# A planned attention and gated feed-forward kernel on one core: weight conversion tied to a row-sum step, and other GpSimd durations in the plan

## The chip, the cores and the metric

The kernel runs on one core of a Trainium2 chip. The metric is the device time in microseconds of one execution, from the runs shown below. One execution was also taken with the hardware profiler, and all rows below come from it.

## The reference

Causal attention over 4 batches, 12 heads, 448 positions and head size 64 gives x with 1792 rows and 768 columns. A feed-forward part follows, with a gate between two matrix products. All data are float32.

```python
scores = q @ k.transpose(0, 1, 3, 2) / sqrt(64)
scores = where(triu(ones((448, 448)), k=1), -1e9, scores)
p = exp(scores - scores.max(-1)); attn = p / (p.sum(-1) + 1e-9)
x = (attn @ v).transpose(0, 2, 1, 3).reshape(1792, 768)
h = x @ w_in                      # 768 x 2048
g = h * clip(h + 3, 0, 6) / 6
out = g @ w_out                   # 2048 x 768
```

## The kernel before

**Groups.** The 1792 positions are worked off in five groups. Group 0 holds the first 112 positions of all four batches (448 columns). Groups 1 to 4 hold the other 336 positions of one batch each. The feed-forward part of a group can start when the attention of its six head pairs is done: every product of its first half reads all six x tiles.

**Attention of group 0** (`first_pair`, six of them, called p = 0 to 5; the row sums of each are its "sums"). For each pair of heads TensorE adds a mask (L321) and the scores (L328), VectorE takes the row maximum (L335, for the second head first), one head's exponential with its row sums is done on ScalarE in four pieces (L347), and the other head goes over VectorE (L355), ScalarE (L359) and a VectorE sum (L362). `inverse` (L368, L369) turns the row sums of both heads into factors, GpSimd multiplies them in (L376), TensorE transposes (L385), ScalarE or VectorE copy the result out (pt), TensorE multiplies by v (L398), and `x_split` writes x as a rounded part xh and a rest xl (ScalarE L237 for xh and for a copy xf; GpSimd or VectorE L249 for xl).

**Attention of the other groups** (`pair`) has the scores (L424), mask and maximum in one VectorE instruction (L441), the exponential (L448), `inverse` (L457, L458), the scaling on GpSimd (`scaled`, L470), transposes (L481) and the product with v (L500).

**Weights** (`weights`). There are 40 chunks: 16 of w_in with 768 columns (three matrix products for each of six 128-column pieces, 18 in all), then 24 of w_out with 512 columns (12 products each). The host sends them as pairs of 32-bit words of a 64-bit array. In group 0 VectorE turns a chunk into float32 with three instructions on half a chunk of 768 columns or on a whole one of 512 (`one_by_one`, L536, L538, L541), by way of a PSUM bank "s" (six banks, shared with the attention). The result wf goes to device memory (`kept`), from which groups 1 to 4 load it. Every chunk is split into wh (ScalarE, L237) and wl (L249, GpSimd or VectorE). The tiles wd (raw words) have 4 buffers, wf, wh and wl 3 each.

**Order.** No order is written out. `Flow` plans it before the program is built: each operation has a key, a list of engines it may run on with a factor on its duration and a lag after which that engine may take it, and the tiles it reads and writes. An engine that is free takes the ready operation with the lowest key whose buffers are free. The resulting order of each engine is then fixed in the program; on the chip every instruction waits for its real inputs. So a duration in the plan is no delay on the chip, it only moves places in the queues. The keys of group 0 that matter here: first pair p starts at -66 + 8p, the sums have that +3.5; the conversion of chunk i has 3i - 9 + .01; the pairs of group 1 start at 4 + 13n.

Of the kernel before, what the change touches and what calls it, by code (L numbers as in the profile page):

```python
# [38 lines left out]
B, H, S, D = 4, 12, 448, 64  # L39
DM, DFF = 768, 2048  # L40
C = 112
NC_ = S // C
R = S - C
NPAIR = H // 2
# [5 lines left out]
T_FIRST, T_EARLY, T_REST, T_LOAD, T_W, T_WLOAD = -66, 4, -16, -24, 9, 9  # L50
# [3 lines left out]
    gh=1, gl=1, prow=3, wf=3, xf=2, r=2, ob=2, qr=3, kr=3, vr=3, wh=3, wl=3, pr3=4, pr2=4, pr1=4,  # L54
# [135 lines left out]
def tile_causal_attention_hardswish_moe(ctx: ExitStack, tc: tile.TileContext, q, k, v, w_in, w_out, out):  # L190
# [11 lines left out]
    flow = Flow({**BUFS, **BANKS})  # L202
# [16 lines left out]
    def one(key, ways, dur, emit, r, w):  # L219

        ways = {e: x if isinstance(x, tuple) else (x, 0) for e, x in ways.items()}
        flow.op(key, ways, [(dur, emit, w)], r)
# [53 lines left out]
    def x_split(key, g, p, av, n):  # L276
        xh, xl = buf("xh", [128, S], F32R), buf("xl", [128, S], F32R)
        x_t[g, p] = xh, xl
        move(key, n, lambda: ap(xh)[:, :n], lambda: ap(av)[:, :n], [(av, 0)], [(xh, 0)], {"A": 1, "D": (1, .5)})
        y = av  # L280
        if g < 2:
            y = buf("xf", [128, S])
            move(key, n, lambda: ap(y)[:, :n], lambda: ap(av)[:, :n], [(av, 0)], [(y, 0)], {"A": 1})
        minus(
            key + .01, n, lambda: ap(xl)[:, :n], lambda: ap(y)[:, :n], lambda: f(ap(xh)[:, :n]),
            [(y, 0), (xh, 0)], [(xl, 0)], {"P": 2, "D": (1, 1.0)} if g < 2 else {"D": 1},
        )


# [6 lines left out]
    def first_pair(p):  # L296
        t = T_FIRST + 8 * p
# [71 lines left out]
            nc.vector.reciprocal(r, r)  # L369

        sums = [(st, 0, 4)] + [(st, 1, 4 + b) for b in range(B)]
        one(t + 3.5, {"D": 1}, .5, inverse, [], sums)
        for e in (1, 0):
            one(
                t + 4, {"P": 1}, 1.05,
                lambda _, e=e: nc.gpsimd.tensor_tensor(  # L376
                    pb[e](), pb[e](), wide(e, 4), ALU.mult
                ),
# [30 lines left out]
    def pair(n):  # L409
        b, p = divmod(n, NPAIR)  # L410
        t = T_REST + 16 * n if b else T_EARLY + 13 * n
# [48 lines left out]
        sums = [(st, e, 4 + i) for e in range(2) for i in TILES]  # L460
        one(t + 4, {"D": 1}, .45, inverse, [], sums)
        pt = {}
        for e in range(2):
            for i in reversed(TILES):
                def scaled(g, e=e, i=i):
                    x, r = ap(pr[e, i]), ap(st)[:, e, 4 + i:5 + i]
                    if g == "A":
                        nc.scalar.activation(x, x, ACTF.Copy, scale=r)
                    else:
                        nc.gpsimd.tensor_scalar(x, x, r, 1.0, ALU.mult, ALU.mult)  # L470
                one(
                    t + 4.5 + .1 * e, {"P": 1}, (C * (i + 1) + 300) / 1100, scaled,
                    [(st, e, 4 + i)], [(pr[e, i], 0)],
                )
            for a, js in enumerate(((0,), (1,), (2, 3))):
                blocks = [(i, j) for j in js for i in range(max(j, 1), NC_)]
                tp, ph = bank("s"), buf(f"pt{js[0]}", [C, S] if js[0] == 0 else [C, R])

                def turn(e=e, blocks=blocks, tp=tp):
                    for o, (i, j) in enumerate(blocks):  # L480
                        nc.tensor.transpose(ap(tp)[:C, C * o:C * o + C], ap(pr[e, i])[:, C * j:C * j + C], ident)  # L481

                key = t + 6 + 3 * e + a
                pe(key, [(.3, turn, [(tp, 0)])], [(pr[e, i], 0) for i in {i for i, _ in blocks}])
                move(
                    key + .1, R, lambda ph=ph: ap(ph)[:, :R], lambda tp=tp: ap(tp)[:C, :R],
                    [(tp, 0)], [(ph, 0)], {"A": 1, "D": (1, .4)} if b else {"A": 1},
                )
                o = 0
                for j in js:  # L490
                    w = R if j == 0 else S - C * j
                    pt[e, j] = ph, o, w
                    o += w
# [18 lines left out]
    def weights(g, i, t, early):  # L512

        n = cols(i)
        wd, wh, wl = buf("wd", [128, 1536], I32), buf("wh", [128, 768], F32R), buf("wl", [128, 768], F32R)
        if g:
            dma(t - T_W - T_WLOAD, 512 * n, lambda: f(ap(wd))[:, :n], lambda: kept[i, :, :n], [("kept", i)], [(wd, 0)])
            w, wk = lambda: f(ap(wd))[:, :n], [(wd, 0)]
        else:
            m, r = divmod(i - NF, 4)  # L520
            src = w_in[i] if i < NF else w_out[m, :, 4 * r:4 * r + 4]
            dma(
                early if early else t - T_W - T_WLOAD, 1024 * n,
                lambda: ap(wd)[:, :2 * n].rearrange("p (n k) -> p n k", k=256), lambda: src, [], [(wd, 0)],
            )
            wf = buf("wf", [128, 768])
            w = lambda: ap(wf)[:, :n]

            def bits(cv, o, m, step):
                ti = ap(cv)[:, :m].bitcast(I32)
                low, high = (ap(wd)[:, 2 * o + a:2 * o + 2 * m:2] for a in range(2))
                if step == 0:
                    nc.vector.tensor_scalar(ti, high, 3, 0x3FFFFFFF, ALU.logical_shift_left, ALU.bitwise_and)  # L536
                elif step == 1:
                    nc.vector.scalar_tensor_tensor(ti, high, -(1 << 30), ti, ALU.bitwise_and, ALU.bitwise_or)  # L538
                else:
                    o = ap(wf)[:, o:o + m].bitcast(I32)  # L540
                    nc.vector.scalar_tensor_tensor(o, low, 29, ti, ALU.logical_shift_right, ALU.bitwise_or)  # L541

            wk = []
            m = n if n <= 512 else n // 2
            for o in range(0, n, m):
                cv = bank("s")
                wk.append((wf, o))
                one_by_one = [
                    (elem(m), lambda _, cv=cv, o=o, a=a: bits(cv, o, m, a), [[(cv, 0)], [(cv, 0)], [(wf, o)]][a])
                    for a in range(3)  # L550
                ]
                flow.op(t - T_W + .01, {"D": (1, 0)}, one_by_one, [(wd, 0)])
            dma(t - T_W, 512 * n, lambda: kept[i, :, :n], w, wk, [("kept", i)])
        move(t - T_W + .1, n, lambda: ap(wh)[:, :n], w, wk, [(wh, 0)], {"A": 1})
        minus(
            t - T_W + .2, n, lambda: ap(wl)[:, :n], w, lambda: f(ap(wh))[:, :n], wk + [(wh, 0)], [(wl, 0)],
            {"D": 1.15, "P": (2, .5)} if g else {"P": 2, "D": (1.15, 2.0)},
        )
        return wh, wl
# [7 lines left out]
    def group(g):  # L567
# [3 lines left out]
        for i in range(NF):  # L571
            t = t0 + 3 * i
            wh, wl = weights(g, i, t, -900 + 4 * i + 11 if not g and i < 4 else None)
            acc, r = bank("mo"), buf("r", [128, S])
            for part in range(3):
                def products(part=part, wh=wh, wl=wl, acc=acc):
                    for c in (2 * part, 2 * part + 1):
                        xh, xl = (ap(x)[:, :n] for x in x_t[g, c])
                        triple(ap(acc)[:, :n], n, wh, wl, c, xh, xl, c == 0, c == NK - 1)
                cs = (2 * part, 2 * part + 1) if g else range(NK)  # L580
                xs = [(x, 0) for c in cs for x in x_t[g, c]]
                pe(t + part, [(step, products, [(acc, 0)])], [(wh, 0), (wl, 0)] + xs)
            t -= 4
            one(
                t, {"A": 1}, (n + 300) / 1200,
                lambda _, r=r, acc=acc: nc.scalar.activation(  # L586
                    ap(r)[:, :n], ap(acc)[:, :n], ACTF.Relu, bias=three, scale=1.0
                ),
                [(acc, 0)], [(r, 0)],
            )  # L590
            def gate(_, r=r, acc=acc):
                nc.vector.scalar_tensor_tensor(ap(r)[:, :n], ap(r)[:, :n], 6.0, ap(acc)[:, :n], ALU.min, ALU.mult)  # L592

            one(t, {"D": 1}, elem(n), gate, [(acc, 0)], [(r, 0)])
            move(
                t, n, lambda i=i: ap(gh)[:, i, :n], lambda r=r: ap(r)[:, :n], [(r, 0)], [(gh, i)],
                {"P": 1.05, "A": (1, .3)} if g else {"A": 1},
            )
            minus(
                t, n, lambda i=i: ap(gl)[:, i, :n], lambda r=r: ap(r)[:, :n], lambda i=i: f(ap(gh)[:, i, :n]),  # L600
                [(r, 0), (gh, i)], [(gl, i)], {"D": 1, "P": (1.9, .7)} if g else {"P": 2, "D": (1, 1.5)},
            )
        for m in range(NK):
            acc, ob = bank("mo"), buf("ob", [128, S])
# [70 lines left out]
```

## Time and profile before

| | us |
|---|---|
| three runs | 676.68, 678.63, 911.4 |
| their median | 678.63 |
| the profiled execution | 676.35 |
| its span (first to last instruction) | 674.6 |
| TensorE busy in the span | 656.7 (97%) |
| VectorE busy | 419.5 (62%) |
| ScalarE busy | 360.6 (53%) |
| GpSimd busy | 236.2 (35%) |

PE stands for TensorE, DVE for VectorE, ACT for ScalarE, POOL for GpSimd. A row of a timeline has the start, the duration, the engine, the line of the program, the operation, output and inputs, and in brackets how long the engine stood idle before it and who ended that. 911.4 is far from the other two runs; the profiled execution is close to them.

### The profile page before, as it was taken

What the parts mean: (1) busy time and instruction counts of PE and PEld (TensorE: products, weight loads), DVE (VectorE), ACT (ScalarE), POOL (GpSimd) and SP (SyncE); (2) the same over time, 40 slices, a digit from 0 to 9 for tenths busy, and PEclk for the clock granted to TensorE, in tenths of its full rate; (3) what the DMA queues carried; (4) which work ended last, traced back from release to release, by engine and by line L of the source; (5) the groups of instructions that cost most, each with busy time, mean ns of one, the idle gap of its engine ahead of it and who ended that gap; (6) DMA issues with size and microseconds to landing.
All of it is one profiled execution on the core that took longest, in us unless ns stands there. A gap on an engine that the chain in (4) does not pass through costs nothing.

```text
span 674.6 us, 11883 instructions
## 1 busy us (share of the span) xinstructions
PE 656.7 (97%) x4236; PEld 573.5 (85%) x4236; DVE 419.5 (62%) x881; ACT 360.6 (53%) x859; POOL 236.2 (35%) x294
## 2 busy tenths in 40 slices
PE   6789999999999999999999999999999999999998
PEld 4558888778888888988988889988898989999997
DVE  5889979995755657444467563455667443466432
ACT  3575666555454556555556565555466654444432
POOL 1556877536651335302242252220335302022000
PEclk7869999999999999999999999999999999999999
DMA  9988777787874343444644335555342334643452
GB/s 225 287 273 241 255 237 229 240 294 236 286 216 146 107 137 114 127 140 130 205 133 131 112 93 161 151 165 176 109 134 85 95 102 133 210 141 111 141 164 70
DMA packets 60347, 113.63 MB, mean 168 GB/s; under 512 B 14976, under 2 KB 26880, under 8 KB 60288
## 3 DMA queue, kind: packets, MB, share of 16 engines
q1 hardware_dynamic: 60288, 112.88, 55.9%
q8 instruction: 33, 0.54, 0.3%
q14 instruction: 26, 0.21, 0.1%
HBM read 94.77 MB, written 18.09 MB: 167 GB/s over the span
## 4 chain that ended last, share of the span: by engine, by line
PE 89%; DVE 4%; POOL 2%; DMA 1%; SPq 1%; issue 1%; ACT 1%; DVEq 0%; ACTq 0%
PE mo L563 24%; PE mo L564 22%; PE mo L565 22%; PE s L424 7%; PE s L500 7%; PE s L481 6%; POOL pr L470 2%; DMA gh<-in_k_dram 1%; SPq L228 1%; DVE s L538 1%; DVE s L536 1%; DVE wl L249 1%; PE s L398 1%; DVE prow L335 0%; PE mo L385 0%
## 5 line engine op out<-in xcount | busy, mean ns | idle before, releaser
L249 DVE TENSOR_TENSOR wl<-wd,wh 128x512 fp32r<-128x512 f32 (+1 forms) x160 | 136.8, 856 | 136.0 <-ACT wh L237 135.7
L237 ACT CAST wh<-wd 128x512 fp32r<-128x512 f32 (+1 forms) x160 | 112.7, 705 | 128.1 <-PE mo L564 78.2
L563 PE MATMUL mo<-xh,wh 128*128 128x336 f32 (+1 forms) x480 | 162.8, 339 | 0.0
L563 PE MATMUL mo<-gh,wh 128*128 128x336 f32 (+1 forms) x480 | 161.6, 337 | 0.0
L565 PE MATMUL mo<-gh,wl 128*128 128x336 f32 (+1 forms) x480 | 156.7, 326 | 0.0
L564 PE MATMUL mo<-gl,wh 128*128 128x336 f32 (+1 forms) x480 | 156.4, 326 | 0.0
L565 PE MATMUL mo<-xh,wl 128*128 128x336 f32 (+1 forms) x480 | 156.4, 326 | 0.0
L564 PE MATMUL mo<-xl,wh 128*128 128x336 f32 (+1 forms) x480 | 156.3, 326 | 0.0
L470 POOL TENSOR_SCALAR pr<-pr,prow 112x224 f32<-112x224 f32 x144 | 98.4, 700 | 118.9 <-PE mo L564 108.6
L563 PEld LDWEIGHTS mo<-xh,wh 128*128 128x128 f32 x480 | 90.1, 188 | 11.7 <-issue 8.8
L244 POOL TENSOR_SCALAR gh<-r 128x336 fp32r<-128x336 f32 x58 | 30.4, 525 | 196.1 <-DVE r L592 175.0
L448 ACT ACTIVATE pr<-s,prow 112x448 f32<-112x448 f32 (+1 forms) x144 | 76.9, 541 | 41.4 <-DVE prow L441 41.2
L563 PEld LDWEIGHTS mo<-gh,wh 128*128 128x128 f32 x480 | 90.2, 188 | 9.7 <-issue 6.7
L565 PEld LDWEIGHTS mo<-gh,wl 128*128 128x128 f32 x480 | 90.2, 188 | 1.5
L564 PEld LDWEIGHTS mo<-gl,wh 128*128 128x128 f32 x480 | 90.3, 188 | 1.3
L565 PEld LDWEIGHTS mo<-xh,wl 128*128 128x128 f32 x480 | 90.1, 188 | 1.5
L564 PEld LDWEIGHTS mo<-xl,wh 128*128 128x128 f32 x480 | 90.3, 188 | 1.1
L441 DVE CUSTOM_DVE_ANT_0 s<-s,mask 112x448 f32<-112x448 f32 (+1 forms) x144 | 69.4, 534 | 21.4 <-PE s L424 21.4
L249 POOL TENSOR_TENSOR wl<-wf,wh 128x512 fp32r<-128x512 f32 (+1 forms) x36 | 54.7, 1519 | 43.2 <-ACT wh L237 41.5
L237 ACT COPY pt<-s 112x336 f32<-112x336 f32 x140 | 53.4, 444 | 23.6 <-PE s L481 23.3
L424 PE MATMUL s<-kr,qr 64*112 64x448 f32 (+2 forms) x288 | 56.8, 492 | 0.5 <-ACT xf L237 0.5
L586 ACT ACTIVATE r<-mo,three 128x336 f32<-128x336 f32 (+1 forms) x80 | 44.5, 557 | 19.7 <-PE mo L565 15.8
(59 smaller groups left out, 674.6 us busy)
## 6 DMA issues: line engine op xcount, KB each, us to landing
wd<-kept_w SPq DMA_DIRECT2D x64, 384.0 KB, 3.3
wd<-kept_w SPq DMA_DIRECT2D x96, 256.0 KB, 2.6
wd<-in_w_in_dram SPq DMA_DIRECT2D x16, 768.0 KB, 5.4
wd<-in_w_out_dram SPq DMA_DIRECT2D x24, 512.0 KB, 5.3
kept_w<-wf SPq DMA_DIRECT2D x16, 384.0 KB, 5.6
kept_w<-wf SPq DMA_DIRECT2D x24, 256.0 KB, 5.6
kr<-in_k_dram SPq DMA_DIRECT2D x24, 224.0 KB, 3.6
vr<-in_v_dram SPq DMA_DIRECT2D x24, 224.0 KB, 3.2
```

Of the source, the lines that this page charges most:

```text
L237: nc.scalar.copy(o(), i()) if scale is None else nc.scalar.mul(o(), i(), scale)
L249: (nc.gpsimd if e == "P" else nc.vector).tensor_tensor(o(), a(), b(), ALU.subtract)
L424: nc.tensor.matmul(ap(ps[e, i])[:C, :w], ap(qr)[m, C * (i - 1):C * i], ap(kr)[m, :w], start=True, stop=True)
L441: lambda _, e=e, i=i, w=w, dst=dst: nc.vector.tensor_tensor_reduce(dst(), dst(), mask[:, S - w:], -0.125, 3.0e38, ALU.add, ALU.min, ap(st) ...
L448: lambda _, e=e, i=i, dst=dst: nc.scalar.activation(ap(pr[e, i]), dst(), ACTF.Exp, bias=ap(st)[:, e, i:i + 1], scale=-1.0, accum_out=ap(st ...
L470: nc.gpsimd.tensor_scalar(x, x, r, 1.0, ALU.mult, ALU.mult)
L481: nc.tensor.transpose(ap(tp)[:C, C * o:C * o + C], ap(pr[e, i])[:, C * j:C * j + C], ident)
L500: nc.tensor.matmul(ap(av)[64 * e:64 * e + 64, R - w:R], ap(vr)[:, j, e, :], ap(ph)[:, o:o + w], start=(j == 0), stop=(j == NC_ - 1),)
L563: nc.tensor.matmul(ps, ap(wh)[:, a], xh, start=start, stop=False)
L564: nc.tensor.matmul(ps, ap(wh)[:, a], xl, start=False, stop=False)
L565: nc.tensor.matmul(ps, ap(wl)[:, a], xh, start=False, stop=stop)
L586: lambda _, r=r, acc=acc: nc.scalar.activation(ap(r)[:, :n], ap(acc)[:, :n], ACTF.Relu, bias=three, scale=1.0),
```

## The change

The `inverse` step of first pair p now counts as the writer of a name ("sums", p). The conversion of every chunk but chunk 0 now counts as a reader of ("sums", 5), so that the plan lets it onto VectorE only once the sums of the last first pair stand before it. No tile is shared between the two, so that the chip itself has no new wait; the order of the queues alone is changed. Five planned durations are changed as well: the xl of groups 0 and 1 on GpSimd (factor 2 to 2.4), the scaling on GpSimd (`scaled`: for 224, 336 and 448 columns from .48, .58, .68 to .65, .87, .95 us), and the rest gl of the gate, on VectorE and GpSimd, with a longer lag before GpSimd may take it in groups 1 to 4.

```diff
@@ x_split
-            [(y, 0), (xh, 0)], [(xl, 0)], {"P": 2, "D": (1, 1.0)} if g < 2 else {"D": 1},
+            [(y, 0), (xh, 0)], [(xl, 0)], {"P": 2.4, "D": (1, 1.0)} if g < 2 else {"D": 1},
@@ first_pair
-        one(t + 3.5, {"D": 1}, .5, inverse, [], sums)
+        one(t + 3.5, {"D": 1}, .5, inverse, [], sums + [("sums", p)])
@@ pair
-                    t + 4.5 + .1 * e, {"P": 1}, (C * (i + 1) + 300) / 1100, scaled,
+                    t + 4.5 + .1 * e, {"P": 1}, min(.95, .2 + C * (i + 1) / 500), scaled,
@@ weights
-                flow.op(t - T_W + .01, {"D": (1, 0)}, one_by_one, [(wd, 0)])
+                flow.op(t - T_W + .01, {"D": (1, 0)}, one_by_one, [(wd, 0)] + ([("sums", NPAIR - 1)] if i else []))
@@ group
-                [(r, 0), (gh, i)], [(gl, i)], {"D": 1, "P": (1.9, .7)} if g else {"P": 2, "D": (1, 1.5)},
+                [(r, 0), (gh, i)], [(gl, i)], {"D": 1.4, "P": (2.6, 1.0)} if g else {"P": 2.3, "D": (1.4, 1.5)},
```

## Rows read from the trace of the kernel before

**Rows 1.** The page: busy tenths of TensorE and its granted clock, 40 slices.

```profile
PE   6789999999999999999999999999999999999998
...
PEclk7869999999999999999999999999999999999999
```

**Rows 2.** Busy time by stretch (us, busy of each engine with count, clock, DMA).

```profile
29.00:51.00 22.00, 15.82 (x93) 9.69 (x94) 19.89 (x48) 14.29 (x44) 11.79 (x11) 0.69 0.91 272
51.00:110.00 59.00, 59.00 (x321) 50.51 (x322) 52.15 (x114) 35.22 (x76) 42.51 (x37) 1.00 0.77 238
...
200.00:670.00 470.00, 468.93 (x3137) 421.49 (x3135) 257.18 (x540) 250.88 (x576) 118.62 (x173) 1.00 0.45 133
```

**Rows 3.** Who TensorE waited for, whole span (total us, times, longest).

```profile
PE s L398 <- ACT pt L237: 4.1, 3, 2.8
...
PE s L481 <- POOL pr L470: 1.1, 4, 0.3
```

**Rows 4.** Timeline of VectorE, 27 to 42 us.

```profile
27.11 1.19 DVE L368 TENSOR_SCALAR prow<-prow 112x8 f32<-112x8 f32 x1
...
30.57 0.55 DVE L536 TENSOR_SCALAR s<-wd 128x384 int32<-128x384 int32 x1
...
32.23 0.62 DVE L249 TENSOR_TENSOR xl<-xf,xh 128x448 fp32r<-128x448 f32 x1
32.76 0.62 DVE L335 TENSOR_REDUCE prow<-s 112x4 f32<-112x448 f32 x1
...
35.50 0.55 DVE L536 TENSOR_SCALAR s<-wd 128x384 int32<-128x384 int32 x1
...
40.47 0.61 DVE L362 TENSOR_REDUCE prow<-pr 112x4 f32<-112x448 f32 x1
41.11 0.17 DVE L368 TENSOR_SCALAR prow<-prow 112x8 f32<-112x8 f32 x1
```

**Rows 5.** Timeline of ScalarE, 33 to 39 us.

```profile
33.70 0.35 ACT L347 ACTIVATE pr<-s,prow 112x112 f32<-112x112 f32 x1 [1.86 <-DVE prow L341]
...
37.77 0.58 ACT L359 ACTIVATE pr<-pr 112x448 f32<-112x448 f32 x1
```

**Rows 6.** Timeline of TensorE, 27 to 51 us, and one row of 95 us.

```profile
27.91 1.04 PE L328 MATMUL s<-gh 64*112 64x112 f32 x16 [0.32 <-DMA gh<-in_k_dram]
...
34.62 1.76 PE L398 MATMUL s<-pt,gl 112*64 112x112 f32 x16 [2.81 <-ACT pt L237]
...
37.24 2.96 PE L424 MATMUL s<-kr,qr 64*112 64x448 f32 x8
...
41.35 0.99 PE L398 MATMUL s<-pt,gl 112*64 112x112 f32 x16 [0.62 <-ACT pt L237]
...
46.66 1.76 PE L398 MATMUL s<-pt,gl 112*64 112x112 f32 x16 [0.62 <-ACT pt L237]
48.35 2.61 PE L424 MATMUL s<-kr,qr 64*112 64x448 f32 x8
50.89 0.47 PE L563 MATMUL mo<-xh,wh 128*128 128x448 f32 x1
...
95.25 1.57 PE L424 MATMUL s<-kr,qr 64*112 64x448 f32 x8
```

**Rows 7.** Timeline of GpSimd, 26 to 28 us.

```profile
26.43 1.84 POOL L249 TENSOR_TENSOR wl<-wf,wh 128x768 fp32r<-128x768 f32 x1 [3.19 <-ACT wh L237]
```

**Rows 8.** Timeline of VectorE: the last instruction of chunk 14's conversion.

```profile
106.15 0.55 DVE L541 SCALAR_TENSOR_TENSOR wf<-wd,s 128x384 int32<-128x384 int32 x1
```

**Rows 9.** Timeline of TensorE: the first product of chunk 14, counted from 50.89 us.

```profile
113.04 0.37 PE L563 MATMUL mo<-xh,wh 128*128 128x448 f32 x1
```

**Rows 10.** Groups of instructions by line and shape (busy us, mean ns | idle before).

```profile
L470 POOL TENSOR_SCALAR pr<-pr,prow 112x448 f32<-112x448 f32 x48 | 43.3, 901 | 0.0
...
L237 ACT CAST wh<-wf 128x768 fp32r<-128x768 f32 x16 | 13.3, 831 | 12.9 <-PE mo L564 11.9 <-DVE wf L541 0.9
...
L249 POOL TENSOR_TENSOR xl<-xf,xh 128x448 fp32r<-128x448 f32 x5 | 6.5, 1293 | 5.0 <-ACT xf L237 5.0
```

## Prediction

> **What bounds the kernel now.** I read the page first. TensorE is at nine tenths or more from the fourth slice on, and the granted clock is at full from the fifth [rows 1]. The table by stretch says the same in numbers: from 51 to 110 us TensorE is busy 59.00 of 59.00 us, and from 200 to 670 us 468.93 of 470.00, at clock 1.00 [rows 2]. After 51 us there is almost nothing to win. The reader is to see that the open time lies ahead of that: from 29 to 51 us TensorE is busy 15.82 of 22.00 us at a mean clock of 0.69, while VectorE is busy 19.89 [rows 2].
>
> The waits of TensorE name who ended its idle time: a pt copy on ScalarE, 4.1 us in three waits, the longest 2.8 [rows 3]. That is no ScalarE problem. In its timeline the exponentials of the last first pair (p = 5) waited 1.86 us for VectorE's L341 until 33.70, and the copy stands behind them [rows 5]. So the third view is VectorE's timeline from 27 to 42 us. The scores of p = 5 are done at 27.91 + 1.04 = 28.95 [rows 6], yet the first of their maxima starts at 32.76, behind a half chunk of conversion from 30.57 to 32.23 and an xl [rows 4]. Three more halves fill 35.50 to 40.47, and only then comes L362, the last row sum, with `inverse` at 41.11 [rows 4]. The first feed-forward product follows at 50.89 [rows 6], 9.78 us later.
>
> **The barrier, part by part.** It takes four half conversions (chunks 1 and 2) from in front of the last sums. One half is 32.23 - 30.57 = 1.66 us, four are 6.64. Chunk 0 stays where it was.
>
> The first half stands alone on the way: without it the maximum starts at 31.1, the exponentials at 33.70 - 1.66 = 32.04, the copy and the product with v behind them equally earlier. The other three are partly hidden. The input of L362 comes from L359, which ScalarE ran from 37.77 to 38.35 [rows 5]; of the three halves only 40.47 - 38.35 = 2.12 stands after that. If ScalarE keeps its order, L359 moves by 1.66 to 36.11 and L362 starts at 36.7: the sums come 1.66 + 2.12 = 3.8 us earlier. If the plan lets L359 run as soon as its input is there (L355 would end near 33.9), the sums come at about 35.2, which is 5.9 earlier. I take 3.8, because the copies that stand ahead of L359 are those of earlier pairs with lower keys (xh of p = 3 has -27.5, L359 of p = 5 has -24). Lower end: 2.1, with another VectorE step or a blocked one in front.
>
> Such a block is in the rows. L368 takes 0.17 us at 41.11, but 1.19 at 27.11, when GpSimd was in a wl from 26.43 to 28.27 [rows 4, 7]. The Trainium skill, "SBUF — State Buffer", section "Who interferes with whom", says that a two-port VectorE instruction and a GpSimd one share a port pair and the second to come waits for the whole of the first; the trace agrees (1.02 us lost). By that rule the last `inverse` may lose the same 1.0 if it falls into an xl on GpSimd, and the gain at the sums would be 2.8.
>
> From the sums to the first product I leave the 9.78 us as they are (scaling, transposes, copy, product with v, xh, xf, xl, in series). So the feed-forward begins near 47.1, 3.8 earlier (2.1 to 5.9). For this to be a gain, the pair products that TensorE runs in between (L424 at 37.24 and 48.35, rows 6) must still fit in; VectorE is free there and fewer banks "s" are taken by conversions, so I count on it.
>
> **What the wait puts off.** Behind the sums now queue the conversions of chunks 1 to 39 and, with each, its write to `kept` on SyncE's queue, the load of a later chunk into the same wd, ScalarE's wh and the wl. After 37.3 the first two chunks cost 6.64 us and end at 43.9 at best, against 40.47 before: a lag of 3.4 us. What hides it is the lead of the conversions. Counted chunk by chunk (18 products for each), the lead is about 10 us for most of the 40 and least for chunk 14: converted at 106.70, first used at 113.04 [rows 8, 9], 6.34 us. From the end of a conversion wh (0.83) and wl (1.84) must follow, 2.9 us with the handing over [rows 7, 10]. Free of cost are thus 6.34 - 2.9 = 3.4 us. VectorE has 59.00 - 52.15 = 6.85 us idle between 51 and 110 us [rows 2], so the lag can be worked off before chunk 14, but TensorE comes 3.8 earlier: 0.4 short if the lag is gone, 3.8 short if none is (then the whole gain is gone). VectorE's idle time is partly waits of its own; I charge 0.9.
>
> **The durations in the plan.** These add no instruction. Measured are 1.29 us for the xl of 448 columns and .90 for the scaling of 448 [rows 10]; the plan had 1.25 and .68 and now has 1.50 and .95. So they err on the long side now. What they can bring is bounded by what TensorE still waits for GpSimd, 1.1 us in four waits [rows 3]. What they can cost is a gl moved to the other engine: hidden, since from 200 to 670 us VectorE is busy 257.18 and GpSimd 118.62 of 470 us [rows 2]. A worse order could cost as much as the four waits, 1.1. I take a gain of 0.3.
>
> **Sum.** -3.8 + 0.9 - 0.3 = -3.2 on the profiled 676.35, which is 673.15. The two runs that lie close to it are 676.68 and 678.63, 0.3 and 2.3 higher, so I add 0.4: 673.5 us. With the bounds of the parts: -5.9 - 1.1 + 0 = -7.0 gives 669.7; -2.1 + 3.4 + 1.1 = +2.4 gives 679.2.
>
> **Rivals.**
> *Filler falls back.* The sums move up, but the pair products that now stand between 37 and 51 us go behind the first chunks. Twelve products of the first pair and eight of the second are about 1.57 us per eight at full clock [rows 6], some 3.6 us in all; then 3.8 - 3.6 leaves nothing: 676.8. The same time comes out if ScalarE's or GpSimd's order, not VectorE's, holds the sums, and the barrier doesn't do what it says. For it: ScalarE had 4.1 us of TensorE's waits. Against it: these waits go back to VectorE, as shown.
>
> *Dense start.* The granted clock there is 0.69. After the wait of 2.81 us, L398 takes 1.76 us where the same work took 0.99 at 41.35; L424 took 2.96 and 2.61 where 1.57 is the time at full clock [rows 6]. Over L398 twice and L424 twice that is .77 + .77 + 1.39 + 1.04 = 4.0 us at the lower of the two levels. If the stage closes up so far that most of its idle 22.00 - 15.82 = 6.2 us and this excess go, up to 10.2 us come back; two thirds of it give 669.9, all 666.5, so I price it at 668. The Trainium skill, "TensorE: Matmul & The Clock Gate", section "What's actually happening", says that the low clock is the default and sustained activity lifts it; that a low stretch follows the 2.81 us wait agrees. Against it: the last scores wait for a DMA until 27.91 whatever VectorE does.
>
> *Starved feed-forward (slower).* The sums gain little, for instance by blocked VectorE steps, and the four halves are pure lag on an engine that is 88% busy. If 6.64 us of lag stay up to chunk 14, the lead of 6.34 turns to -0.3, and TensorE waits 2.9 + 0.3 = 3.2 us there: 679.6. A wait of 2.81 us was followed by a slow L398 and a slow L424, .77 + 1.39 = 2.2 us more [rows 6]: 681.8. I price it at 681. It decides from a lag of 3.4 us at chunk 14. Against it: the 6.85 us of idle VectorE.
>
> **How the numbers follow.** Forecast 0.52, filler falls back 0.20, dense start 0.12, starved 0.13, and 0.03 for an order that I don't foresee. The range reaches to the priced end of the dense start and to just short of the starved case's: 667.5 to 680.5. A measurement of this kernel tells about 2%, 13.6 us, from no change. The ceiling of 10.2 us is below that, and so is the starved case; faster by over 2% 0.03, within 0.94, slower 0.03.
>
> **What would show it.** Right: no L536 between chunk 0 and the last L362; `inverse` of p = 5 near 37 instead of 41.1; the first L563 near 47; TensorE full from there. Clock from 29 to 47 us above 0.69. If chunk 14 or a neighbour makes TensorE wait for wl, wh or wf, the starved case is at work. If L563 starts early with more L424 behind it than before, the filler fell back. The forecast is wrong if another engine's order turns out to hold the last sums, or if the new order delays pairs and chunks in later groups, where TensorE now waits for almost nothing.

## The result and the profile after

The changed kernel takes 669.0 us (667.65 to 671.1, four runs) beside 677.65 before. Of the four runs behind 677.65 one took 911.4 us and is left out of the ratio, which is 0.9886 with a 95% interval from 0.9842 to 0.993. Timed a second time beside some of the experiments it took 669.19, ratio 0.9893 (0.9875 to 0.9911). By this second ratio the change makes the kernel 7.2 us or 1.1% faster. The time is inside the stated range, and the gain is more than twice the 3.2 us that the prediction added up. Its profiled execution took 668.97 us with a span of 667.3.

The page of the changed kernel answers to [rows 1]:

```profile
PE   7689999999999999999999999999999999999998
...
PEclk9989999999999999999999999999999999999999
```

The clock is now at nine tenths or more in all slices but the third. Busy time by stretch, as in [rows 2], and the stretch from 29 to 60 us:

```profile
29.00:51.00 22.00, 17.61 (x116) 13.45 (x117) 19.66 (x45) 13.76 (x38) 14.92 (x12) 0.84 0.92 281
51.00:110.00 59.00, 58.78 (x320) 48.54 (x320) 55.13 (x119) 35.79 (x80) 37.76 (x37) 1.00 0.78 238
...
200.00:663.00 463.00, 463.00 (x3107) 417.53 (x3106) 255.32 (x546) 251.09 (x577) 109.16 (x157) 1.00 0.45 134
...
29.00:60.00 31.00, 26.40 (x158) 21.24 (x159) 28.31 (x63) 18.75 (x49) 21.46 (x17) 0.89 0.91 278
```

TensorE's waits, as in [rows 3]:

```profile
PE mo L385 <- POOL pr L376: 4.1, 4, 2.4
...
PE s L398 <- ACT pr L448: 1.8, 1, 1.8
...
PE mo L563 <- DVE r L592: 0.2, 1, 0.2
```

The 1.1 us that TensorE waited for the scaling on GpSimd in the later groups have gone. VectorE, as in [rows 4]:

```profile
29.14 0.61 DVE L249 TENSOR_TENSOR xl<-xf,xh 128x448 fp32r<-128x448 f32 x1
29.68 0.62 DVE L335 TENSOR_REDUCE prow<-s 112x4 f32<-112x448 f32 x1
...
34.44 0.61 DVE L362 TENSOR_REDUCE prow<-pr 112x4 f32<-112x448 f32 x1
35.09 0.17 DVE L368 TENSOR_SCALAR prow<-prow 112x8 f32<-112x8 f32 x1
...
35.41 0.54 DVE L536 TENSOR_SCALAR s<-wd 128x384 int32<-128x384 int32 x1
```

ScalarE, as in [rows 5]:

```profile
33.56 0.60 ACT L359 ACTIVATE pr<-pr 112x448 f32<-112x448 f32 x1
36.19 0.53 ACT L237 CAST xh<-s 128x448 fp32r<-128x448 f32 x1 [2.03 <-PE s L398]
```

TensorE, as in [rows 6]:

```profile
32.02 2.96 PE L424 MATMUL s<-kr,qr 64*112 64x448 f32 x8
...
39.15 0.64 PE L424 MATMUL s<-kr,qr 64*112 64x224 f32 x4
...
42.11 1.64 PE L398 MATMUL s<-pt,gl 112*64 112x112 f32 x16 [1.80 <-ACT pr L448]
43.68 0.74 PE L563 MATMUL mo<-xh,wh 128*128 128x448 f32 x1
```

What to see: no conversion stands among the VectorE steps of the last first pair; the last `inverse` starts at 35.09 instead of 41.11; L359 goes ahead of xh, the order that I had not taken; the first feed-forward product starts at 43.68 instead of 50.89, 7.21 us earlier. It does so with 12 pair products (L424) ahead of it, where before had 20; the missing eight are 1.57 us of work at full clock [rows 6], so coming 7.21 us earlier is worth 5.6. From the first product on, TensorE's idle time is 0.22 + 0.44 + 0 = 0.66 us (51 to 110, 110 to 200 and 200 to 663 us) against 0.49 + 1.07 = 1.56 before. The sum of 5.6 and 0.9 is 6.5 of the 7.3 by which the spans differ.

By the trace alone the story of the prediction would pass: the barrier freed the sums, the clock and the idle time came back as in its "dense start". The experiments say otherwise about what freed the sums.

### The profile page after: what moved, and what is told of

Same layout as the page of the kernel before. It is cut to its first block, busy times and chain, and to the rows that moved or that the text cites. A ratio compares the mean times of both kernels' runs of the same rounds, so it can differ in the third digit from the quotient of the medians.

```text
span 667.3 us, 11888 instructions
## 1 busy us (share of the span) xinstructions
PE 650.2 (97%) x4236; PEld 569.6 (85%) x4236; DVE 419.3 (63%) x890; ACT 364.3 (55%) x869; POOL 222.2 (33%) x275
## 4 chain that ended last, share of the span: by engine, by line
PE 92%; DVE 4%; DMA 1%; ACT 1%; issue 1%; POOL 1%; SPq 0%; DVEq 0%; POOLq 0%; ACTq 0%
PE mo L563 25%; PE mo L564 23%; PE mo L565 23%; PE s L424 8%; PE s L500 7%; PE s L481 6%; DVE s L538 1%; DVE s L536 1%; DMA gh<-in_k_dram 1%; DVE wf L541 1%; POOL pr L376 1%; PE s L398 0%; PE s L328 0%; DVE prow L335 0%; PE mo L385 0%
## 5 line engine op out<-in xcount | busy, mean ns | idle before, releaser
L249 DVE TENSOR_TENSOR wl<-wd,wh 128x512 fp32r<-128x512 f32 (+1 forms) x156 | 131.3, 841 | 146.7 <-ACT wh L237 146.5
L563 PE MATMUL mo<-xh,wh 128*128 128x336 f32 (+1 forms) x480 | 163.3, 340 | 0.2 <-DVE r L592 0.2
L563 PE MATMUL mo<-gh,wh 128*128 128x336 f32 (+1 forms) x480 | 161.2, 336 | 0.0
L470 POOL TENSOR_SCALAR pr<-pr,prow 112x224 f32<-112x224 f32 x144 | 100.6, 715 | 125.8 <-PE mo L564 112.7
L448 ACT ACTIVATE pr<-s,prow 112x448 f32<-112x448 f32 (+1 forms) x144 | 77.3, 542 | 40.8 <-DVE prow L441 40.8
L563 PEld LDWEIGHTS mo<-xh,wh 128*128 128x128 f32 x480 | 90.4, 188 | 9.8 <-issue 5.4
L563 PEld LDWEIGHTS mo<-gh,wh 128*128 128x128 f32 x480 | 90.2, 188 | 9.6 <-issue 6.9
L244 POOL TENSOR_SCALAR gh<-r 128x336 fp32r<-128x336 f32 x51 | 25.8, 506 | 188.5 <-DVE r L592 172.7
L441 DVE CUSTOM_DVE_ANT_0 s<-s,mask 112x448 f32<-112x448 f32 (+1 forms) x144 | 70.2, 531 | 26.4 <-PE s L424 26.4
L249 POOL TENSOR_TENSOR wl<-wf,wh 128x512 fp32r<-128x512 f32 (+1 forms) x33 | 50.1, 1518 | 39.8 <-ACT wh L237 32.2
L586 ACT ACTIVATE r<-mo,three 128x336 f32<-128x336 f32 (+1 forms) x80 | 44.6, 557 | 24.7 <-PE mo L565 24.7
L424 PE MATMUL s<-kr,qr 64*112 64x224 f32 (+2 forms) x288 | 54.4, 483 | 0.0
```

The lines of the kernel that those rows point to most:

```text
L249: (nc.gpsimd if e == "P" else nc.vector).tensor_tensor(o(), a(), b(), ALU.subtract)
L424: nc.tensor.matmul(ap(ps[e, i])[:C, :w], ap(qr)[m, C * (i - 1):C * i], ap(kr)[m, :w], start=True, stop=True)
L441: lambda _, e=e, i=i, w=w, dst=dst: nc.vector.tensor_tensor_reduce(dst(), dst(), mask[:, S - w:], -0.125, 3.0e38, ALU.add, ALU.min, ap(st) ...
L448: lambda _, e=e, i=i, dst=dst: nc.scalar.activation(ap(pr[e, i]), dst(), ACTF.Exp, bias=ap(st)[:, e, i:i + 1], scale=-1.0, accum_out=ap(st ...
L563: nc.tensor.matmul(ps, ap(wh)[:, a], xh, start=start, stop=False)
L586: lambda _, r=r, acc=acc: nc.scalar.activation(ap(r)[:, :n], ap(acc)[:, :n], ACTF.Relu, bias=three, scale=1.0),
```

## The experiments

All were timed beside the kernel before, whose medians on the three occasions were 676.12, 676.32 and 676.51. Gains against the kernel before are named by the ratio, differences between two of the other kernels by their medians; the two ways differ by up to 0.9 us (the durations alone gain 3.1 us by the ratio and 3.6 by the medians). "Idle" is TensorE's idle time from 29 us to the last product, "clock" its mean granted clock from 29 to 60 us. "Loss" is idle plus 31 us times the shortfall of the clock; it is a rough account, since it counts a low clock also where TensorE is idle. "L424" counts the pair products ahead of the first L563. Idle, clock and moments are of one profiled execution each. The same kernel's moments differ by about 1 us between executions (the last inverse of the changed kernel at 35.09 and at 36.23).

| kernel | median us | ratio (95%) | last inverse | first L563 | L424 | idle | clock | loss |
|---|---|---|---|---|---|---|---|---|
| before | 676.3 | 1 | 41.1 | 50.9 | 20 | 7.7 | .78 | 14.5 |
| barrier alone | 675.58 | .9993 (.9977 to 1.0009) | 39.9 | 44.5 | 12 | 8.7 | .83 | 13.9 |
| durations alone | 672.49 | .9954 (.9937 to .9972) | 37.0 | 44.5 | 12 | 8.1 | .89 | 11.5 |
| changed, chunk 1 free | 672.61 | .9952 (.9937 to .9968) | 37.5 | 44.5 | 12 | 8.2 | .83 | 13.5 |
| changed, chunk 0 bound too | 671.68 | .9947 (.9921 to .9973) | 37.6 | 43.2 | 12 | 5.3 | .89 | 8.7 |
| xl factor alone | 673.91 | .9961 (.9946 to .9976) | 36.8 | 43.4 | 12 | 6.6 | .82 | 12.2 |
| barrier and xl factor | 671.56 | .9922 (.9902 to .9943) | 36.5 | 45.1 | 12 | 6.5 | .89 | 9.9 |
| changed, old xl factor | 673.41 | .9946 (.9928 to .9964) | 39.9 | 44.5 | 12 | 7.6 | .83 | 12.9 |
| barrier, mask first | 671.68 | .9926 (.9909 to .9943) | 40.2 | 48.6 | 24 | 6.3 | .83 | 11.5 |
| changed, again | 669.19 | .9893 (.9875 to .9911) | 36.2 | 43.8 | 12 | 6.7 | .94 | 8.6 |
| changed, mask first | 669.05 | .9890 (.9873 to .9908) | 36.2 | 45.8 | 24 | 5.6 | .94 | 7.5 |
| durations, mask first | 670.48 | .9911 (.9895 to .9928) | 38.0 | 48.7 | 20 | 5.9 | .86 | 10.2 |
| changed, late conversion | 667.29 | .9866 (.9846 to .9885) | 36.0 | 44.0 | 20 | 4.0 | .94 | 5.9 |

The profiled times minus the loss lie between 659.6 and 662.4 us for all of these kernels, while the times themselves spread over 9.3 us. So TensorE's idleness and low clock behind 29 us account for most of the differences; the moment of the last sums alone does not ("barrier, mask first" has it at 40.2, and its median is 4.6 us below that of the kernel before).

**Barrier alone.** The durations as before:

```diff
+        one(t + 3.5, {"D": 1}, .5, inverse, [], sums + [("sums", p)])
+                flow.op(..., one_by_one, [(wd, 0)] + ([("sums", NPAIR - 1)] if i else []))
```

> The barrier without the five changed durations. Theory A (the barrier brings the last sums forward, and nearly all of the gain lies ahead of the first feed-forward product): the last inverse near 35 to 36 us instead of 41.1, the first L563 near 44 to 45 instead of 50.9, 670 to 671 us; the waits of TensorE for GpSimd in the later groups (1.1 us) come back. Theory B (the durations do it, by another order on GpSimd and ScalarE): little change, 675 to 677. Theory C (the granted clock of the start differs from execution to execution and makes up much of the difference): 671 to 674, with a time that follows the mean clock of the runs.

No change that can be measured. That sinks theory A for the barrier by itself. Theory C, the granted clock of each execution, can be judged by the runs on record. Of the 47 runs of the kernel before that were timed beside the experiments, the 15 with a mean granted clock of 0.99 or more have a median of 675.0 us, the other 32 one of 676.6. The five runs of the changed kernel on the last occasion all have 0.99 or more and a median of 669.19, so that 5.8 us of its gain are left at a like clock. It is not shown whether the rest is chance or the higher clock is itself brought by the change. With the barrier alone the nine runs at 0.99 or more have a median of 675.6, no gain at all. VectorE of this kernel:

```profile
33.14 0.58 DVE L355 TENSOR_TENSOR pr<-s,prow 112x448 f32<-112x448 f32 x1
35.18 0.62 DVE L240 CAST xh<-s 128x448 fp32r<-128x448 f32 x1 [1.46 <-PE s L398]
36.93 0.63 DVE L441 CUSTOM_DVE_ANT_0 s<-s,mask 112x448 f32<-112x448 f32 x1 [1.13 <-PE s L424]
...
39.25 0.61 DVE L362 TENSOR_REDUCE prow<-pr 112x4 f32<-112x448 f32 x1
39.90 0.17 DVE L368 TENSOR_SCALAR prow<-prow 112x8 f32<-112x8 f32 x1
...
50.73 0.51 DVE L441 CUSTOM_DVE_ANT_0 s<-s,mask 112x336 f32<-112x336 f32 x1
...
51.51 0.60 DVE L536 TENSOR_SCALAR s<-wd 128x384 int32<-128x384 int32 x1
...
54.45 0.55 DVE L541 SCALAR_TENSOR_TENSOR wf<-wd,s 128x384 int32<-128x384 int32 x1
54.92 0.61 DVE L592 SCALAR_TENSOR_TENSOR r<-r,mo 128x448 f32<-128x448 f32 x1
```

The places that the conversions left are taken by steps that wait for TensorE (1.46 and 1.13 us), and the last sums come only 1.2 us earlier. Then six half conversions bunch from 40.63 to 50.73 in front of the next mask step L441. ScalarE and TensorE pay for it (timeline):

```profile
51.34 0.54 ACT L448 ACTIVATE pr<-s,prow 112x336 f32<-112x336 f32 x1 [2.97 <-DVE prow L441]
51.87 0.82 ACT L237 CAST wh<-wf 128x768 fp32r<-128x768 f32 x1
52.59 0.64 ACT L586 ACTIVATE r<-mo,three 128x448 f32<-128x448 f32 x1
...
55.59 0.74 PE L563 MATMUL mo<-xh,wh 128*128 128x448 f32 x1 [3.08 <-DVE r L592]
```

and its stretch from 29 to 60 us, where TensorE is busy 23.18 of 31 us:

```profile
29.00:60.00 31.00, 23.18 (x135) 17.54 (x136) 26.80 (x61) 17.24 (x48) 19.29 (x16) 0.83 0.78 243
```

The exponential L448 waits for the mask step; the L586 that reads the bank of the first chunk's products stands behind it in ScalarE's fixed order; the gate L592 follows; and the third chunk's products wait 3.08 us for one of the two banks "mo". The gate itself stands behind two more half conversions, from 51.51 us on, and starts 1.7 us after L586 has ended at 53.23, so that part of the wait is due to these.

**Durations alone.** The changed kernel without the barrier:

```diff
-                flow.op(..., one_by_one, [(wd, 0)] + ([("sums", NPAIR - 1)] if i else []))
+                flow.op(..., one_by_one, [(wd, 0)])
```

> The five durations without the barrier. Theory A: the last inverse stays near 41, the first L563 near 50; only the 1.1 us of waits for GpSimd in later groups go: 675 to 676.5. Theory B: 669 to 671, with early sums. Theory C: 672 to 677.

3.1 us faster than before, with the last sums 4 us earlier and two half conversions (chunk 1) still ahead of them. Theories A and B both miss this. The time lies within theory C's range, but its runs above and below a clock of 0.99 have the same median (672.40 and 672.50). The durations do more for the sums than the barrier, but give only part of the gain. VectorE and TensorE of this kernel:

```profile
34.73 0.55 DVE L536 TENSOR_SCALAR s<-wd 128x384 int32<-128x384 int32 x1
...
36.38 0.61 DVE L362 TENSOR_REDUCE prow<-pr 112x4 f32<-112x448 f32 x1
37.02 0.66 DVE L368 TENSOR_SCALAR prow<-prow 112x8 f32<-112x8 f32 x1
...
54.08 0.47 PE L563 MATMUL mo<-xh,wh 128*128 128x448 f32 x1 [1.99 <-DVE r L592]
```

One half (34.73) now stands where three stood, and the wait for the bank is there again, 1.99 us.

**Changed, chunk 1 free.**

```diff
-                ... + ([("sums", NPAIR - 1)] if i else []))
+                ... + ([("sums", NPAIR - 1)] if i > 1 else []))
```

> The changed kernel, but chunk 1 as well as chunk 0 is free to be converted ahead of the sums (two half conversions of 1.66 us more ahead of them). Theory A: the sums come 1.7 to 3.3 us later than with the full barrier, and 670 to 672 us. If only the place of the half ahead of the last maximum matters, all of the 3.3 show. Theory B: as the changed kernel, 669. Rival within A: the halves fall into idle time of VectorE, and nothing is lost: 669.

672.61 against 669.19: freeing one chunk costs 3.4 us, the whole of what the barrier adds to the durations (672.49 against 669.19). The start is that of the durations alone (last inverse at 37.5, first product at 44.5, a wait of 2.0 us for the bank).

**Changed, chunk 0 bound too.**

```diff
-                ... + ([("sums", NPAIR - 1)] if i else []))
+                ... + ([("sums", NPAIR - 1)]))
```

> The changed kernel with chunk 0 behind the barrier as well, so that no conversion at all stands ahead of the sums. Theory A: the sums come 0 to 1.5 us earlier (the last scores wait for a DMA until about 27), the conversions lag by up to 3.3 us more; the least lead from a conversion to its first product in the changed kernel is 4.7 us (chunk 10), which would fall to some 1.4, less than the 2.9 us that wh and wl need, so TensorE waits 1 to 2 us there: 669 to 671. If the lead is refilled, 667 to 668.

2.5 us slower than the changed kernel, a little beyond the expected span, and not for the expected reason. The sums came later, not earlier, and no wait for weights is to be seen, although chunk 0 is now converted only 1.9 us ahead of its first product. TensorE's first stretch of products from 43 to 47 us ran at the lower level (clock 0.50), which a 1.76 us L398 at 41.47 precedes. The trace shows where the sums lose time, much as with the barrier alone: ScalarE waits 0.97 us for an xh that VectorE makes and runs the last L359 at 35.93 instead of 33.56, and VectorE puts two mask steps and a copy in front of the last L362. Why the plan chooses this order was not followed up.

**The xl factor alone.** The other durations belong to operations that come later (the first scaling L470 starts at 54.87 us in the kernel before), so that of the five this one should be what shapes the start:

```diff
-            [(y, 0), (xh, 0)], [(xl, 0)], {"P": 2, "D": (1, 1.0)} if g < 2 else {"D": 1},
+            [(y, 0), (xh, 0)], [(xl, 0)], {"P": 2.4, "D": (1, 1.0)} if g < 2 else {"D": 1},
```

> The kernel before with one number changed: the planned GpSimd factor of xl, 2 to 2.4. Theory D (this one duration sets the order of the first 45 us, because the other changed durations belong to operations that the plan starts later): the last inverse near 37 and the first L563 near 44.5, as with all five durations; waits for GpSimd in later groups as before; 672 to 674 us. Rival E (the durations of the scaling and of gl do it): 675 to 677.

As theory D has it: 673.91, last inverse at 36.8, and waits for the scaling of 1.0 us as before. The wait of L563 for the bank is there too, 1.8 us.

```profile
36.82 0.66 DVE L368 TENSOR_SCALAR prow<-prow 112x8 f32<-112x8 f32 x1
```

**Barrier and xl factor.** The barrier's two lines and the xl line above, nothing else.

> The barrier and the xl factor 2.4, the other durations as before. Theory D: the start is that of the changed kernel (last inverse near 35.1, first L563 near 43.7, no long wait of L563 for L592), and about 1 us of waits for GpSimd in the later groups comes back: 669 to 671. Rival E: as with the barrier alone, 675.

671.56. No wait of L563 for L592 was left, and the sums came at 36.5 in an execution whose earlier steps ran 0.5 to 1.0 us late (its first and fifth `inverse` started at 13.24 and 32.68 where the changed kernel has 12.72 and 31.66). The scaling and gl durations thus bring the remaining 2 us or so, as they do without the xl factor (675.58 with the barrier alone, 673.41 in the next run); 0.8 of it are the waits for L470.

**Changed, old xl factor.** The changed kernel with the xl line put back.

> The changed kernel with the xl factor back at 2. Theory D: the start is that of the barrier alone (last inverse near 39.9, first L563 near 44.5, L563 waits about 3 us for L592), the later groups without waits for GpSimd: 673.5 to 675. Rival E: as the changed kernel, 669.

673.41 with a last inverse at 39.9 and the long wait, as theory D has it:

```profile
55.62 0.47 PE L563 MATMUL mo<-xh,wh 128*128 128x448 f32 x1 [3.10 <-DVE r L592]
```

**Barrier, mask first.** To test the chain L441, L448, L586, L592 by itself, the mask step of the first pair of group 1 gets a key ahead of the conversions:

```diff
-                        t + 2 * j + .1, {"D": 1}, elem(w) + .2,
+                        t + 2 * j + .1 if n else -10, {"D": 1}, elem(w) + .2,
```

> The barrier alone, and the mask step L441 of the first pair of group 1 with a key ahead of the conversions (-10 instead of 4.1 and 6.1), so that it does not queue behind six half conversions. Theory F (with the barrier alone L563 waits 3.1 us for L592 because the conversions bunch in front of L441, the exponential L448 waits for L441, and the L586 that empties the product's bank stands behind L448 on ScalarE): the wait falls below 1 us, and 672 to 673.5 us. Rival G (the gate L592 is late of itself, behind conversions on VectorE): the wait stays and the time is 675 to 676.

671.68, 3.9 us less than the barrier alone, by this one key. The wait for the bank is gone, although the sums are no earlier:

```profile
40.17 0.17 DVE L368 TENSOR_SCALAR prow<-prow 112x8 f32<-112x8 f32 x1
...
41.71 0.43 DVE L441 CUSTOM_DVE_ANT_0 s<-s,mask 112x224 f32<-112x224 f32 x1
...
45.16 3.54 PE L424 MATMUL s<-kr,qr 64*112 64x448 f32 x12
48.63 0.47 PE L563 MATMUL mo<-xh,wh 128*128 128x448 f32 x1
```

TensorE does 24 pair products ahead of the first L563 and then does not wait once up to 200 us. The first L563 is 4.1 us later than with the barrier alone, and the time 3.9 shorter: an early first product is worth little if filler is left undone and a later product waits. That is theory F; the two halves in front of L592, shown above, are the part that rival G had right.

**Changed, again.**

> The changed kernel itself, timed beside the next three. All theories: 668 to 671 us, as before.

669.19, as stated above; this is the reference for the next three. In this execution L563 waited 1.3 us for L592.

**Changed, mask first.** The key of -10 in the changed kernel.

> The changed kernel with the mask step L441 of the first pair of group 1 ahead of the conversions. Theory F (the time is the sum of what TensorE loses by idleness and low clock, and the changed kernel loses only 0.2 us at the product's bank): nothing left to win there, 668.5 to 671, within 1 us of the changed kernel. Rival G (an earlier mask step is worth its own 4 us, as with the barrier alone): 665 to 667.

669.05: theory F, within 1 us. But its loss is 1.1 us lower than that of the run beside it, and that does not show in the time, so the sum of theory F is good to about 1 us only. Waits for conversions (L424 for L541, 0.8 us) come in place of those for the bank.

**Durations, mask first.** The key of -10 in the kernel with the durations alone.

> The five durations without the barrier, with the mask step first. Theory F: the 2.0 us wait of L563 for L592 goes, 670 to 671 us, so that the barrier is worth no more than 1 to 2 us on top. Rival H (the barrier is needed for the whole gain): 672 to 673.

670.48: theory F again; 2.0 us less than the durations alone. With the mask key in place of the barrier the durations bring 6.0 of the 7.2 us. So the barrier is one way, and not the only one, to get rid of the wait for the bank.

**Changed, late conversion.** Chunks 1 to 4 get a lag of 5 us in the plan after the sums:

```diff
-                flow.op(t - T_W + .01, {"D": (1, 0)}, one_by_one, ...
+                flow.op(t - T_W + .01, {"D": (1, 5.0 if 0 < i < 5 else 0)}, one_by_one, ...
```

> The changed kernel with chunks 1 to 4 held back in the plan for 5 us more after the last sums. The starved case of the prediction: the least lead of the changed kernel is 4.7 us (chunk 10) against 2.9 needed, so 1.8 us are free; of 5 us of lag some are made good because the mask steps go first: TensorE waits 0 to 3 us for weights, 669.5 to 673 us. Rival (the lead does not matter, because idle time of VectorE refills it): 668 to 669.5.

667.29, faster than both kernels and 1.9 us faster than the changed one (its slowest run, 668.03, is below the other's fastest, 668.73). Neither the starved case nor "no effect" came true. Its VectorE and TensorE, in the timeline:

```profile
35.96 0.17 DVE L368 TENSOR_SCALAR prow<-prow 112x8 f32<-112x8 f32 x1
...
39.77 0.60 DVE L536 TENSOR_SCALAR s<-wd 128x384 int32<-128x384 int32 x1
...
40.84 0.99 PE L398 MATMUL s<-pt,gl 112*64 112x112 f32 x16 [0.73 <-ACT pt L237]
41.76 2.33 PE L424 MATMUL s<-kr,qr 64*112 64x448 f32 x8
```

and its stretch from 29 to 60 us:

```profile
29.00:60.00 31.00, 27.79 (x171) 22.19 (x172) 28.15 (x66) 19.53 (x53) 21.79 (x19) 0.94 0.86 263
```

The conversions start 3.8 us after the sums, behind all the mask steps of the first pair. The last L398 no longer waits 1.80 us for a bank "s" that an L448 holds, eight more pair products fit ahead of the first L563, and TensorE is busy 27.79 of 31 us instead of 26.40 (24.73 in the changed kernel's second execution). Nor does an L424 wait here for a bank that a conversion holds, as it does for 0.8 us in "changed, mask first". Counted as in the prediction, the leads of chunks 1 to 7 fall to between 4.4 and 5.5 us, still above the 2.9 us that the prediction took as needed, and TensorE waits for no weights.

## Why the prediction was right in direction and off in size

The direction was right and the time lies in the range, but the mechanism was wrong: the barrier that was to bring the gain brings none by itself, and some 3.3 us (672.49 to 669.19) only on top of the durations, which were held for almost nothing. That the range holds the result is partly luck. The bounds of the sum's own parts end at 669.7, just above the 669.0 and 669.19 measured; the range reached lower because of the "dense start".

- *Where the time is open* was right: behind the first product 0.9 of the 7.3 us came back, in the start 5.6; 0.8 is not placed.
- *The barrier brings -3.8* was the step that failed. By itself it brings 0.5 us (0.9993, interval across 1). The four halves did go from in front of the sums; that the VectorE steps behind them would then move up was assumed, and in the plan other steps that wait for TensorE took the places. The loss behind the first product (3.08 us at the bank "mo") took what was left.
- *The durations bring -0.3* failed with it. Alone they bring 3.1, and on top of the barrier 6.4 (675.58 to 669.19). I had bounded them by the waits for GpSimd that the trace shows, 1.1 us. That bounds the operations themselves. It does not bound what another duration does to the order of all engines: the xl factor moved the last `inverse` by some 4 us (41.1 to 36.8) without any work changed. The sum allowed the durations 1.1 us at most, either way.
- *ScalarE keeps its order*, hence 3.8 rather than 5.9: wrong for the changed kernel (L359 at 33.56, sums 6.0 us earlier). With the barrier alone L359 does run at 36.32, near the 36.11 of the prediction, but the last L362 follows only at 39.25 instead of 36.7. I had put down to the barrier an order that the xl factor decides.
- *9.78 us from the sums to the first product*: 8.59 in the changed kernel, 4.6 with the barrier alone, 8.5 with the mask first. It is no constant, as TensorE's fillers stand in it. Nor does the first L563 wait for all six x tiles on the chip, as the description of the groups has it: with the barrier alone it starts at 44.49, while the last L398, whose result is the sixth x tile, runs from 43.57 to 44.56.
- *The charge of 0.9 for a shorter lead* was not due. The change's least lead, counted the same way, is 4.7 us (chunk 10) and no wait for weights followed. The late conversion shows that leads of 4.4 to 5.5 us for chunks 1 to 7 cost nothing either. The lead was deep because the conversions are early, not because the products need it.
- *Rivals.* "Dense start", 668 with a chance of 0.12, names the size that came, and by the traces idle and low clock did come back (the loss fell from 14.5 to 8.6 us); that the barrier would bring this did not hold. "Filler falls back" happened in part, 1.57 us. The starved case came in no run: no lead behind chunk 0 fell below the 2.9 us, so what a shorter one costs is not measured.
- *A blocked L368* did not occur at the last sums (0.17 us; 0.66 with the durations alone), but removing the conversion brought another meeting: VectorE's xl moved to 29.14, and the two scalings L376 on GpSimd from 28.80 on took 2.64 us instead of 1.83, TensorE's L385 waiting 2.37 for them. In all eight profiles in which this xl stands beside the two scalings (the kernels with the barrier that leaves chunk 0 alone free) they took 2.64 or 2.65 us; in the other six 1.82 to 1.86. The Trainium skill, "SBUF — State Buffer", section "Who interferes with whom", says that a VectorE instruction with two SBUF inputs contends with a GpSimd one that reads SBUF; the trace agrees. GpSimd before, then GpSimd and TensorE of the changed kernel (the xl of 29.14 is shown above):

```profile
29.33 1.83 POOL L376 TENSOR_TENSOR pr<-pr,prow 112x448 f32<-112x448 f32 x2
...
28.80 2.64 POOL L376 TENSOR_TENSOR pr<-pr,prow 112x448 f32<-112x448 f32 x2
...
30.61 0.60 PE L385 MATMUL mo<-ident,pr 112*112 112x112 f32 x4 [2.37 <-POOL pr L376]
```

Open: by which steps of the plan the xl factor turns the order, why binding chunk 0 makes the sums later, what share of the last 2 us comes from scaling and what from gl, and 0.8 us of the changed kernel's gain.

## What to carry to other kernels

In a planned kernel a planned duration is an input like any other: bound it by the stage whose order it can shape, not by the waits that its operation causes, and test the parts of a change one by one, since here two parts worth 0.5 (within the noise) and 3.1 us are worth 7.2 together. Moving work off a queue only helps if what moves up is ready; look at what takes the freed places, and at which later step then stands behind the moved work (here the mask step that through three engines releases a product's bank). Filler that is off the path may well be best as late as its consumers allow: the best kernel here is the one that keeps the conversions back longest behind the last sums (3.8 us). That is one run, and other lags were not tried.

## What the runs showed of the hardware

The granted clock of the first 29 us differs between executions of almost the same order, and no effect on the progress is to be seen: it was 0.76 before and 1.00 in the changed kernel, with the third `inverse` at 19.28 and 19.25 us. Over all profiles the third `inverse` starts at 18.79 to 19.83 in the five with a clock of 0.76 to 0.88, and at 19.25 to 20.17 in the nine with 1.00. In that stretch of the kernel before TensorE waits 3.5 us for transfers of q and k and 2.3 us for VectorE's first steps. The stretch of the kernel before:

```profile
0.00:29.00 29.00, 21.97 (x180) 17.34 (x180) 19.62 (x44) 13.98 (x47) 9.95 (x15) 0.76 1.02 253
```

and that of the changed kernel:

```profile
0.00:29.00 29.00, 20.22 (x180) 15.20 (x180) 20.87 (x46) 14.64 (x52) 10.43 (x16) 1.00 1.02 263
```

TensorE's busy time there is no sign of the clock: 21.97 us for 180 matrix products at 0.76, 20.22 at 1.00, but 22.50 at 1.00 in the second execution of the changed kernel.

The mean of 0.90 us for the scaling of 448 columns [rows 10] mixes two cases. In the kernel before 26 of the 48 took 0.63 to 0.67 us and 22 took 1.06 to 1.68; beside each of the 22, and for at least 0.56 us, VectorE ran a subtraction (L249), beside the others for 0.43 at most. Not every such meeting costs: three scalings of the changed kernel with 0.56 or 0.57 us of it beside them took 0.64. So the old planned duration of .68 fits the undisturbed scaling, and the new one of .95 the mean.
